# A searched instruction order is replaced by another: engine queues, eviction engines and buffer addresses of a two-branch kernel

## The chip, the cores and the metric

The kernel runs on one core of a Trainium2 chip. The metric is the device time of one execution in microseconds (us), the median of several runs. Inside the core, TensorE (PE) multiplies, VectorE (DVE) and ScalarE (ACT) evict results from the accumulators (PSUM, eight banks) and do elementwise work, GpSimd (POOL) does some elementwise work on the on-chip memory (SBUF), and SyncE (SP) issues nearly all transfers. Each engine works through a queue of its own, strictly in order; semaphores tie the queues together.

## The reference, cut to what matters

Two independent branches over 2048 rows and 576 columns are computed and put side by side.

```python
# branch A: short convolution, product, long convolution over the sequence, gate
k_shift = sum(k_pad[:, t:t+S] * shift_k[:, ks-1-t] for t in range(4))
kv = k_shift * v
y  = irfft(rfft(pad(kv)) * rfft(pad(ssm_k)))[:, :S] + kv * ssm_D
a  = q * y
# branch B: linear attention, 32 heads of 18 columns
qkv = x @ wqkv;  pq, pk = phi(q), phi(k)      # phi(t) = t+1 or exp(t), + 1e-6
o   = (pq @ (pk^T v)) / (pq @ sum(pk) + 1e-6)
b   = o @ wo
out = concat([a, b], axis=-1)
```

## The kernel before, in words

Branch A runs the long convolution as a hand-built Fourier transform in matmuls, in three column pieces (`cc`) of 192, for the filter (`h`) and the data (`u`). Filter columns are transposed on TensorE (`htr`, line 453) and evicted (`hev`); `one1` and `srow` make the four tap rows by matmul (`wjm`, line 314, evicted by `wjev`). VectorE and GpSimd form `kv` (`tap`, `tap+`, `tapv`). `s1` (line 494) is the first transform stage, evicted as 128x768 blocks (`s1ev`, tiles Ch and Cu). Each of the nine 64-column pieces (of the filter and of the data) then has a 32x32-block transpose on VectorE (`tr`, line 533) and two `s2` blocks of eight 32x32-tile matmuls each (line 544): the first block of a piece uses two of the four row groups of the weights, the second the other two. Evictions are 128x1024 (`s2ev`, tiles sph and spu). For each piece a swapped copy X of the filter spectrum is made by two transfers, then come two products of 2048 columns (`p2` on X, `p1` on sph), the inverse stage `i1` (line 590, evicted by `i1ev` into V), a sum and a difference (`vs`, `vd`) and the last stage `i2` (line 633, 24 blocks of four matmuls), whose result is multiplied with q and written out (`yo`); some of these blocks are first copied out of PSUM (`yev`) and then multiplied in SBUF (`yq`), others are multiplied straight out of PSUM (`i2q`).

Branch B projects keys (`k`, line 681, 16 blocks) and queries (`q`, line 703), applies phi in an exponential on ScalarE (`kexp`, `qexp`) and a combination on VectorE (`kphi`, `qphi`), accumulates x^T pk (`G`, line 749; evictions `gcol` and `Gev`), goes through a small chain (`kv`, `z`, `den`, `rden`, a round trip through DRAM `rw`, `rr`) to normalise the queries (`pqn`), folds the output weights into M (line 844), and ends in 16 `out` blocks (line 886; o0 to o7, two of each) that are evicted (`oev`, tile ob) and written out (`oo`). A `fill` (line 921) is two 512-column matmuls on a constant that nobody reads; there are 18.

The order of all this is not written in the Python code. Every operation gets a number as it is declared; the text PLAN lists all 711 numbers, each with the letter of its engine (P, A, D, G for POOL, S for SP), and each engine's queue is the sequence of its words. The text PLACES gives every buffer its SBUF address or PSUM bank in order of declaration. `_issue` reads both:

```python
    for w in PLAN.split():
        o = P.ops[int(w[1:])]
        o.eng = names[w[0]]
        order.append(o)
    ...
    for b, p in zip([b for b in P.bufs if b.space != "dram"], places, strict=True):
        b.pos = p
```

Two rules follow from this. A transfer or a write into an address waits for all earlier users of that address, so PLACES creates waits too. And a two-operand product on GpSimd carries a wait for the last such product that stands before it in VectorE's queue (flag `two`), so that the two engines take turns with products. The three small loads (idw is number 16, Drow 20, srow 23) are declared with ScalarE as their only engine, in the code that both versions share, and they are the first three words of ScalarE's queue in both PLANs (A16, A23, A20).

Numbers that are used below: 360, 357, 355, 352, 350 and so on are `s2` blocks; 693 to 710 fills; 315 the last `out` block and 316 its eviction, 317 its transfer out; 686 and 688 the last `i2` blocks; 489 and 550 the products on X of pieces 2 and 5; 476 and 478 the two `i1` blocks of piece 1; 548 and 549 the two copies X of piece 5; 105 a load of half of q; 480 the sum `vs` of piece 1; 101 a `tapv` of 1536 columns.

Of the kernel before, what the change touches and what calls it, by code (L numbers as in the profile page):

```python
# [946 lines left out]
A16 A23 A20 G692 P697 G10 G5 P708 P706 P695 G7 S318 G218 G0 P702 G24 G8 G71 G1 P321 P25 D26 S324 P701 G3 G12 P319 P29  # L947
P328 G11 P27 P325 S364 S19 D320 A30 A329 A28 P367 P365 P696 D330 D327 A326 G4 D322 S51 P347 D366 P345 D346 A368 P374
A348 A375 P337 A338 G6 G369 P339 G331 S18 D340 P700 G332 G323 P335 P341 D342 A336 P333 P343 A334 P384 P31 D344 D359
D349 G13 P707 A385 P380 S50 P370 G52 A32 P372 A381 S53 P360 A361 G2 D371 S54 P150 P382 A373 G64 S58 S60 A151 G57 S56  # L950
S59 S36 S35 G37 S55 D354 P153 S61 P378 A15 A383 P376 S63 A377 D152 S41 A379 A154 D78 S66 S17 S40 P147 G79 P144 P108
A148 S62 D155 A145 D149 S46 D146 D391 P357 P159 P362 A109 D110 A358 P350 D396 A160 D161 S67 A363 P156 P397 S45 P352
S72 D82 A351 A353 A157 P111 D158 A398 G42 G9 P167 P164 A112 D113 P123 S68 G83 P129 D80 A168 D169 D386 A165 D166 P355
A124 D125 A130 G81 A356 P117 S48 P394 S43 D131 S74 A118 P392 A393 G14 D90 G47 P183 A395 P446 A184 P114 D119 P126 A447
D84 D85 D185 A115 A127 P138 A139 S75 P132 D128 G91 D116 P440 D140 P448 G44 A133 D134 P141 P442 A441 S70 D449 A49 A142
A443 D143 P450 P120 D98 A451 P438 S38 P436 S401 P135 A439 A437 P444 P180 A121 S65 A136 G92 D122 P399 G93 A445 A181
P387 D137 A388 A400 D482 S33 P172 P186 D467 P178 D182 P468 A173 P175 S69 D452 S402 A187 A469 D174 S73 A179 P389 A390
G34 G39 P470 A471 D86 D87 P203 P453 G99 P455 A176 P208 D177 A456 P170 A204 G213 A205 P162 P211 P509 S403 A454 A171
A209 P503 A163 A210 P511 A212 P223 D94 D224 A504 D225 P188 D88 A512 P485 P483 D89 A510 P226 P505 S214 D189 S77 S76
A484 D227 P228 D190 D506 S457 G404 S458 P415 A486 D229 P705 G100 P419 P411 A416 A420 S232 P501 S233 A502 P230 S215  # L960
S473 D412 P497 A498 P499 P507 A508 A500 D95 D96 D97 P191 G101 S472 S487 P413 P417 P409 D231 A192 P206 S488 D528 A414
S239 S241 S243 P405 S22 A410 D207 D459 S237 P558 S246 S245 A418 P407 D474 A408 S217 A559 A406 P193 P560 S234 A561 D489
D475 P568 A194 D460 A195 P566 A567 P198 D242 P531 A569 P529 S216 A199 D421 P196 G244 D543 P562 A532 A530 S235 S252
A197 P422 S250 P424 A200 P201 A425 S248 A423 P570 P564 S254 D490 D563 P544 A202 G238 P220 G240 D426 S548 D513 S256
A571 P546 A565 D222 A545 G219 S533 P572 D221 G236 P429 A547 P709 A430 S580 D573 P266 P516 A267 D431 S534 P262 D517
P476 A263 D604 G249 P698 P260 A477 P434 D435 A261 P264 A265 P258 A259 P427 D574 A428 P493 S519 S518 S247 A494 P461
P463 D462 A464 P268 P478 P432 A269 D589 G251 G253 P575 P279 S549 A479 S107 D433 A576 A280 P491 A492 P285 D536 A286
D257 P592 A593 D255 P514 D535 P270 P300 D551 S106 A515 P605 S610 A271 S579 A301 D465 S287 D520 D521 A606 P607 A608
S594 P273 S595 D480 A274 P282 D481 P590 D495 D550 A283 P577 P294 A591 S302 S609 D596 D611 A578 S281 D496 P524 A525
A295 P297 D582 P522 A298 P537 A538 P288 A523 D597 P539 A540 D612 A289 S21 P276 P552 D526 P554 A277 P306 A553 A555 P613  # L970
P291 A614 S103 A307 S105 S272 P615 S290 A292 D541 S284 S299 S296 D466 P633 D542 A634 D556 P627 P621 P639 P631 P619
S102 S278 A616 D527 D557 A632 P637 A622 D581 P625 S104 A638 G635 A620 P661 D628 P655 P657 S308 D640 P600 D662 D626
A656 P598 S275 A658 P585 S663 A601 D617 P309 S293 P583 D629 D623 S636 A599 S624 D659 S660 D618 D641 A586 S642 D602
P312 S630 D603 P664 A584 P651 D587 D588 P649 A310 S311 D665 D666 P645 P643 A313 A652 A650 A646 S314 A644 P674 S667
# [19 lines left out]
"""  # L994


# [28 lines left out]
```

## Time and profile before

| what | value |
|---|---|
| median of three runs | 153.41 us (152.92 to 153.5) |
| the profiled execution | 153.26 us, of which the span is 151.5 us |
| PE / DVE / ACT / POOL busy | 146.9 / 134.6 / 125.9 / 60.8 us |
| granted TensorE clock | 1.0 |
| transfers | 35.37 MB, mean 234 GB/s |

The span is the time from the first to the last instruction on the trace; about 1.8 us lie outside it. Busy time says how long an engine had an instruction in execution, not whether the engine was the one that others waited for. Matmul records overlap, since matmuls are pipelined; the chain of waits counts each moment once, so its durations of matmul groups are used for what such a group costs. Group lists give the mean duration of one instruction by shape.

### The profile page before, as it was taken

Reading aid. Unit: us, or ns where it says so; the run is one execution under the profiler, and the core shown is the slowest. Engines: PE = TensorE matmul, PEld = TensorE weight load, DVE = VectorE, ACT = ScalarE, POOL = GpSimd, SP = SyncE. Lnnn points to the kernel's source line nnn. Section 1 sums busy time; section 2 is a strip of 40 time slices with the busy share of each in tenths; the row PEclk is TensorE's granted clock in tenths of the full one; section 3 lists DMA queues with packets and bytes.
Section 4 is the critical chain, followed back from the end, with each engine's and each line's share of the span. In section 5 each row is a group of like instructions: output and inputs, shape, how many; then the busy total and the mean of one; then the engine's idle time right before and its main releaser. Section 6 shows DMA issues by size and latency. Waiting matters only on the chain.

```text
span 151.5 us, 4023 instructions
## 1 busy us (share of the span) xinstructions
PE 146.9 (97%) x1627; PEld 110.4 (73%) x1627; DVE 134.6 (89%) x145; ACT 125.9 (83%) x174; POOL 60.8 (40%) x57
## 2 busy tenths in 40 slices
PE   7999999999999999999999999999999999999992
PEld 2568587566768886657867887675777799999970
DVE  0157999999999989999999999999999999999930
ACT  3069888797798788999889879999999999999930
POOL 8107313943911945951063430699940000040200
PEclk9999999999999999999999999999999999999999
DMA  4999999999999791799992776976676796599892
GB/s 132 404 321 254 164 228 286 220 210 176 239 338 296 215 205 34 223 297 196 374 297 57 294 235 162 308 224 253 205 191 262 245 345 169 162 304 244 238 248 89
DMA packets 52629, 35.37 MB, mean 234 GB/s; under 512 B 43328, under 2 KB 48321, under 8 KB 52482
## 3 DMA queue, kind: packets, MB, share of 16 engines
q1 hardware_dynamic: 51918, 33.49, 79.7%
q0 software_dynamic: 544, 1.57, 5.7%
q8 instruction: 13, 0.21, 0.6%
q10 hardware_dynamic: 148, 0.05, 0.2%
q14 instruction: 6, 0.05, 0.1%
HBM read 19.64 MB, written 5.77 MB: 168 GB/s over the span
## 4 chain that ended last, share of the span: by engine, by line
PE 85%; ACT 9%; DVE 2%; issue 2%; POOL 0%; ACTq 0%; POOLq 0%
PE ps_all L681 15%; PE ps_all L703 12%; PE ps_all L886 12%; PE ps_all L749 11%; PE ps_all L494 9%; PE ps_all L921 6%; PE ps_all L590 5%; PE ps_all L633 5%; PE ps_all L544 4%; PE ps_all L453 2%; ACT spu L235 2%; ACT sph L235 2%; PE ps_all L314 2%; ACT Cu L235 1%; ACT M L235 1%
## 5 line engine op out<-in xcount | busy, mean ns | idle before, releaser
L248 POOL TENSOR_TENSOR m<-m 128x3072 bf16<-128x3072 bf16 (+1 forms) x4 | 18.2, 4562 | 14.7 <-DVE m L417 8.6
L681 PE MATMUL ps_all<-wk,xT 128*128 128x324 bf16 x160 | 23.7, 301 | 0.0
L886 PE MATMUL ps_all<-M,pqT 126*128 126x288 bf16 (+1 forms) x160 | 22.1, 287 | 0.1
L681 PEld LDWEIGHTS <-xT 128*128 128x128 bf16 x160 | 17.8, 113 | 4.4 <-issue 0.7
L417 DVE TENSOR_TENSOR m<-kh,Wj 128x6144 bf16<-128x6144 bf16 x6 | 20.1, 3346 | 0.0
L886 PEld LDWEIGHTS <-pqT 126*128 126x128 bf16 (+1 forms) x160 | 17.2, 114 | 2.5 <-issue 1.1
L703 PE MATMUL ps_all<-xT,wq 128*126 128x512 bf16 x80 | 18.7, 382 | 0.0
L494 PEld LDWEIGHTS <-Gsb 128*128 128x128 bf16 x192 | 16.2, 98 | 3.3 <-issue 1.1
L248 POOL TENSOR_TENSOR pqT<-pqT,rb 126x1024 bf16<-126x1024 bf16 (+1 forms) x7 | 14.8, 2133 | 7.7 <-DVE pqT L248 6.5
L235 ACT ACTIVATE spu<-ps_all 128x1024 bf16<-128x1024 f32 x17 | 16.9, 1029 | 0.7 <-PE ps_all L544 0.7
L235 ACT ACTIVATE V<-ps_all 128x1024 bf16<-128x1024 f32 x17 | 17.2, 1116 | 0.0
L235 ACT ACTIVATE Cu<-ps_all 128x768 bf16<-128x768 f32 x20 | 16.3, 858 | 1.1 <-PE ps_all L681 0.6
L749 PE MATMUL ps_all<-pk,x_sb 128*128 128x288 bf16 (+1 forms) x128 | 17.1, 287 | 0.0
L235 ACT ACTIVATE sph<-ps_all 128x1024 bf16<-128x1024 f32 x16 | 15.9, 1023 | 1.1 <-PE ps_all L544 0.8
L235 ACT ACTIVATE Ch<-ps_all 128x768 bf16<-128x768 f32 x18 | 14.3, 852 | 1.9 <-PE ps_all L494 1.8
L703 PEld LDWEIGHTS <-wq 128*126 128x126 bf16 x80 | 10.4, 136 | 6.4 <-issue 1.1
L749 PEld LDWEIGHTS <-x_sb 128*128 128x128 bf16 x128 | 12.1, 98 | 3.8 <-issue 0.9
L686 ACT ACTIVATE ek<-ps_all,neg 128x648 bf16<-128x648 f32 x16 | 12.4, 806 | 2.8 <-PE ps_all L681 2.7
L248 POOL TENSOR_TENSOR q<-yb,q 128x768 bf16<-128x768 bf16 (+1 forms) x2 | 2.6, 1280 | 29.4 <-DVE yb L237 22.2
L689 DVE SCALAR_TENSOR_TENSOR pk<-ek,ps_all 128x648 bf16<-128x648 bf16 x16 | 12.7, 823 | 0.8 <-ACT ek L686 0.8
L921 PE MATMUL ps_all<-cft 128*128 128x512 bf16 x36 | 11.4, 449 | 1.0 <-POOL cft L915 1.0
L235 ACT ACTIVATE ob<-ps_all 128x576 bf16<-128x576 f32 x16 | 10.4, 724 | 1.9 <-PE ps_all L886 1.7
(95 smaller groups left out, 299.5 us busy)
## 6 DMA issues: line engine op xcount, KB each, us to landing
X<-sph SPq DMA_DIRECT2D x18, 256.0 KB
kh<-in_A_k_dram SPq DMA_DIRECT2D x6, 384.0 KB
v<-in_A_v_dram SPq DMA_DIRECT2D x6, 384.0 KB
x_sb<-in_B_x_dram SPq DMA_DIRECT2D x4, 576.0 KB
q<-in_A_q_dram SPq DMA_DIRECT2D x6, 384.0 KB
out_dram<-ob SPq DMA_DIRECT2D x16, 144.0 KB
out_dram<-q SPq DMA_DIRECT2D x11, 192.0 KB
rb<-r_scr SPq DMA_DIRECT2D x8, 252.0 KB
```

The costliest lines, as they stand in the source:

```text
L235: nc.scalar.activation(out=o, in_=i, func=ACTF.Copy)
L248: return (nc.vector if e == "DVE" else nc.gpsimd).tensor_tensor(out=o, in0=a, in1=b, op=op)
L417: return nc.vector.tensor_tensor(out=m.t[:], in0=i0, in1=i1, op=ALU.mult)
L494: nc.tensor.matmul(ps.t[:, bank, lo - 384 * bank:hi - 384 * bank], lhsT=Gsb.t[:, b, ri, :], rhs=src[:, lo - CC * j:hi - CC * j], start=Tru ...
L590: nc.tensor.matmul(view(ps.t[:], 128 * c + 16 * wi, [[32, 4], [1, 16]]), lhsT=src.t[:, 4 * h0 + c, :], rhs=Ei.t[:, 0, 64 * wi:64 * wi + 64 ...
L681: nc.tensor.matmul(ps.t[:, hh, 0:KH], lhsT=cols(xT.t[0:KT[t], t, :], r), rhs=wk.t[0:KT[t], t, KH * hh:KH * hh + KH], start=(t == 0), stop= ...
L686: P.op("A", lambda e: nc.scalar.activation(out=eb.t[:], in_=ps.t[:, :, 0:KH], func=ACTF.Exp, bias=neg1.t[:]), rd=[ps, neg1], wr=[eb], name ...
L689: P.op("D", lambda e: nc.vector.scalar_tensor_tensor(out=pk[r // 4].t[:, r % 4, 0:2 * KH].rearrange("p (h c) -> p h c", h=2), in0=eb.t[:], ...
L703: nc.tensor.matmul(ps.t[0:hn, c - c0, :], lhsT=wq.t[0:KT[t], t, HCH[c][0]:HCH[c][0] + hn], rhs=xT.t[0:KT[t], t, :], start=(t == 0), stop=( ...
L749: nc.tensor.matmul(ps.t[0:m, 0, 0:n], lhsT=x4[r // 4].t[:, r % 4, :] if t == 4 else x_sb[r // 4].t[:, r % 4, 128 * t:128 * t + 128], rhs=p ...
L886: nc.tensor.matmul(ps.t[:, hh - h, 0:HALF], lhsT=cols(pqT[r // 8].t[0:hn, c, 512 * (r // 4 % 2):512 * (r // 4 % 2) + 512], r), rhs=M.t[0:h ...
L921: nc.tensor.matmul(fps.t[:, 0, :], lhsT=cft.t[:], rhs=view(cft.t[:], 0, [[0, 4], [1, 128]]), start=True, stop=True)
```

## The change

Both texts are replaced; no other line changes. The same 711 operations are issued, on the same data and with the same shapes. What differs is the order inside each engine's queue, the engine of 40 operations, and the buffer addresses. The lines that matter most, cut:

```diff
 PLAN = """
-A16 A23 A20 G692 P697 G10 G5 P708 P706 P695 G7 S318 G218 G0 P702 G24 G8 G71 G1 P321 P25 D26 S324 P701 G3 G12 P319 P29
-P328 G11 P27 P325 S364 S19 D320 A30 A329 A28 P367 P365 P696 D330 D327 A326 G4 D322 S51 P347 D366 P345 D346 A368 P374
...
-P476 A263 D604 G249 P698 P260 A477 P434 D435 A261 P264 A265 P258 A259 P427 D574 A428 P493 S519 S518 S247 A494 P461
...
-S594 P273 S595 D480 A274 P282 D481 P590 D495 D550 A283 P577 P294 A591 S302 S609 D596 D611 A578 S281 D496 P524 A525
...
-D653 D647 P680 D681 P682 P676 P670 S654 P688 P686 D675 A683 S648 A677 A689 P303 P668 P315 P694 G684 A671 S685 D678
-P703 D690 D672 D687 A304 S679 S691 P693 S305 D669 S673 P704 A316 S317 P710 P699
+G692 P700 G10 P701 P702 P696 D24 S318 G3 G71 P707 A16 G6 A23 S324 S19 P321 G12 P29 S364 D322 S51 D30 P319 P697 P328
+P31 A20 G57 D329 P325 D330 D326 A320 G323 S18 G331 G1 S50 D327 G64 A32 P706 P339 A340 S53 P337 S54 S58 P345 P367 A346
...
+P476 P434 D435 P478 P709 P266 A477 A479 P427 S252 S105 S549 S247 A267 P546 A428 A547 S548 D589 P461 D462 P268 A269
...
...
+D628 D629 A671 P682 P676 S305 S314 D669 P674 D672 D681 P688 A683 A677 D684 A665 P686 A689 S630 S673 S685 P315 D675
+D678 D687 D690 D666 S679 S691 S667 D316 P693 P699 P703 P698 P710 P694 P704 S317
```

The operations that change engine:

| from, to | operations |
|---|---|
| ACT to DVE | `hev` 3, `wjev` 2, `oev` 2 (277 and 316), `Gev` 2, `yev` 2, `gcol`, `s2ev` of u (545), `s1ev` of h 2 |
| DVE to ACT | `s1ev` of h 5, `s1ev` of u 2 (449 and 563), `yev` 3, `Gev` 2, `hev` |
| DVE to POOL | `p2` (489), `vs` (480), `pqn` 2, `yq` |
| POOL to DVE | `tapv` (101), `one1` (24), `pqn` 2, `yq` 2 (635, 684) |
| ACT to POOL | `x4c` (a small copy) |

The `s2` blocks stand in TensorE's queue, from first to last, in these groups without other work between:

```
before: 360 | 357 | 362 350 | 397 352 | 355 | 394 392 | 399 387 | 468 | 389 470 | 453 455 | 485 483 | 531 529
        | 422 424 | 544 | 546 | 429 | 516 | 434 | 427 | 432 575 | 592 514 | 605 607 | 590 577
after:  360 357 | 362 350 | 397 352 | 394 392 | 355 | 399 387 | 470 468 | 389 453 | 483 455 | 485 | 531 424 529
        | 544 422 | 429 | 516 | 434 | 427 546 | 432 | 607 514 | 592 590 | 605 | 577 575
```

Of the fills, twelve stand ahead of the last `out` block before and eleven after; five open TensorE's queue in both.

More of the change, by code (lines that the diff above doesn't have):

```diff
@@ L952 @@
[L952 to L961, printed above, removed]
@@ new lines @@
+A398 G83 A157 P352 P167 D158 S63 A353 A168 P129 P123 A130 D80 D169 P164 S48 D386 A124 P111 G5 G81 D131 D125 A165 P446
+G14 D166 P117 P394 A112 A447 D113 P392 A393 S45 A395 P183 P438 A118 D90 P114 S75 D119 D84 S74 A439 D85 A184 P355 G47
+D185 P126 A356 G91 A115 G49 D116 A127 D128 P132 S43 A133 S401 P138 A139 P448 A449 S73 D134 P141 D140 G13 A142 P440
+A441 D143 P444 P120 P450 P442 A445 D98 A451 P135 A443 S70 P436 G92 A15 G93 G9 A121 A136 A437 P180 P399 A181 D122 P387
+A388 D137 D467 P172 P705 D452 A400 S33 S38 S72 A173 P470 D182 D482 S69 D174 D86 P468 A471 S402 P175 P389 A469 P453
@@ new lines @@
+P592 D574 S533 A283 P590 A289 P276 A593 P605 A591 D277 G480 P306 P577 A606 A307 S107 P575 S519 A576 S594 P554 P270
+P291 A555 A271 P552 S102 D535 P294 D596 D536 A578 D520 A292 D481 D495 D521 A553 A295 S579 D556 S609 P537 A538 P539
+A540 S21 P309 P522 S284 D597 A310 S610 A523 P524 A525 D581 D582 P463 S103 D557 S281 A464 P297 S290 S278 D526 S106 P300
+S104 D496 D465 P600 A298 P585 D466 A301 P285 A586 P583 S311 P631 A601 D611 A584 S296 P633 S293 P273 A632 A634 A286
+S299 S302 S272 D541 S287 D527 D542 D612 P639 D587 P661 P637 P621 A640 A274 D635 A638 P598 D622 S275 P655 P657 P649
```

29 lines of the change are left out of this document (15 added, 14 removed), and 30 rows, old and new, of the table PLACES.

## The prediction, on record before the result

> **What bounds the kernel now.** I read the page first (busy shares), then busy time in stretches, then the chain of waits, then the groups by shape.
>
> ```profile
> span 151.5 us, 4023 instructions
> ...
> PE 146.9 (97%) x1627; PEld 110.4 (73%) x1627; DVE 134.6 (89%) x145; ACT 125.9 (83%) x174; POOL 60.8 (40%) x57
> ```
>
> ```profile
> 16.00:76.00 60.00, 59.97 (x524) 42.69 (x523) 59.01 (x49) 51.96 (x68) 28.75 (x18) 1.00 1.01 231
> 76.00:100.00 24.00, 23.56 (x292) 18.11 (x291) 23.83 (x25) 21.04 (x31) 10.60 (x5) 1.00 0.73 230
> 100.00:144.00 44.00, 43.69 (x679) 37.42 (x678) 43.72 (x62) 43.30 (x64) 14.01 (x9) 1.00 0.76 235
> ```
>
> The columns of the stretches are length, then busy time (and instructions) of PE, PEld, DVE, ACT and POOL, the clock, the share of the transfer engines and GB/s. From 16 to 144 us VectorE works 126.6 of 128 us: it has no slack. ScalarE has 8.0 us of slack up to 76, 3.0 in the next 24 and only 0.7 in the last 44. TensorE is busy throughout too, but a busy PE may be one whose next matmul is held back, so I take its share from the chain of waits (start, duration, what):
>
> ```profile
> 1.01 4.45 PE ps_all L921 x10
> ...
> 26.48 0.34 PE ps_all L544 x8
> ...
> 29.12 0.36 PE ps_all L544 x16
> ...
> 65.65 0.55 PE ps_all L544 x16
> ...
> 144.49 0.33 PE ps_all L633 x4
> 144.82 1.24 PE ps_all L886 x10
> 146.06 2.59 PE ps_all L921 x12
> ```
>
> The real work of TensorE begins behind the first fills, at 5.46, and ends at 146.06; the last 2.59 us of fills delay nobody. So three engines are nearly full at once, and no single one can be relieved to great effect. A new order can win only what lies in waits, in fills ahead of 146.06, and in the way blocks follow each other.
>
> **The change part by part.** The work is the same, so I count what the order does to each queue. All sums are against the profiled execution (153.26 us: the span of 151.5 and 1.76 around it); it lies 0.15 below the median of 153.41, so 0.15 is added at the end.
>
> *TensorE, the s2 blocks.* A block of eight alone takes 0.34 us. Two neighbours that use different row groups take 0.36 together (29.12); two that use the same row groups take 0.55 (65.65: blocks 389 and 470, both second halves). In the old order ten blocks stand alone, eleven pairs mix halves and two pairs (389 470, 432 575) do not: 10 x 0.34 + 11 x 0.36 + 2 x 0.55 = 8.46 us. In the new one seven stand alone, twelve pairs mix, one pair (544 422) does not, and three stand in a row (531 424 529: 0.55 + 0.03, since the third mixes with the second): 7 x 0.34 + 12 x 0.36 + 0.55 + 0.58 = 7.83. That removes **0.63 us** where TensorE sets the pace, nothing where it waits anyway; I take it whole, as it is spread over the run.
>
> *TensorE, the fills.* A fill is 2.59 / 6 = 0.43 us. Eleven stand ahead of the last out block, one fewer: **-0.43 us**, if the fill filled no wait; if it did, 0. The seven at the end take 3.0 us behind block 315 and end before the last transfer lands, so they cost nothing.
>
> *VectorE.* The prices are the mean ns in these groups:
>
> ```profile
> L248 DVE TENSOR_TENSOR X<-spu,X 128x2048 bf16<-128x2048 bf16 x9 | 11.1, 1263 | 0.0
> ...
> L237 DVE CAST Ch<-ps_all 128x768 bf16<-128x768 f32 x6 | 5.6, 940 | 0.8 <-PE ps_all L494 0.7
> L248 DVE TENSOR_TENSOR VS<-V 128x896 bf16<-128x896 bf16 x9 | 5.5, 616 | 0.0
> ...
> L248 DVE TENSOR_TENSOR v<-m,v 128x1536 bf16<-128x1536 bf16 x3 | 2.9, 959 | 0.1
> L248 DVE TENSOR_TENSOR q<-ps_all,q 128x384 bf16<-128x384 f32 x5 | 2.7, 552 | 0.2
> L237 DVE CAST sph<-ps_all 128x1024 bf16<-128x1024 f32 x2 | 2.4, 1178 | 0.0
> ...
> L248 DVE TENSOR_TENSOR q<-yb,q 128x384 bf16<-128x384 bf16 x4 | 1.3, 367 | 0.0
> ...
> L237 DVE CAST Wj<-ps_all 128x576 bf16<-128x576 f32 x1 | 0.8, 758 | 6.8 <-PE ps_all L314 6.8
> ```
>
> Behind the first block transposes, where VectorE is full, it loses two Ch evictions (371, 412; 2 x 0.94), two of Cu (449, 563; the same shape as Ch), p2 489 (1.26), vs 480 (0.62) and one yev net (128x384 from PSUM, 0.55 as the q row), 6.2 us. It gains one spu eviction (545, priced as the sph row, 1.18), two of ob (277, 316; 128x576 from PSUM as Wj, 2 x 0.76), tapv 101 (0.96) and 0.37 us of yq, 4.0 us. Small ones (gcol, Gev, pqn) cancel within 0.2. Net **about -2 us of VectorE work**. The additions ahead of the transposes (one1, two wjev, two hev net, against two s1ev) lie ahead of 16 us, where at most 134.6 - 126.6 = 8 us of VectorE's work stands; I take 0 for them, with 0 to +0.4 as bounds, since the transposes there wait for the last eviction of s1 and one more wjm block (0.6) now stands before that, and one htr block is taken later.
>
> *ScalarE.* An ob eviction is this row:
>
> ```profile
> L235 ACT ACTIVATE ob<-ps_all 128x576 bf16<-128x576 f32 x16 | 10.4, 724 | 1.9 <-PE ps_all L886 1.7
> ```
>
> In the full last 44 us ScalarE gives away two of these (1.4) and one 128x1024 eviction (at most the 1.18 of the row above), and takes one 128x768 (at most 0.94) and one 128x384 (at most 0.55): about 1 us less, bounds 0.5 to 1.5. The rest of its changes lie earlier, in its slack.
>
> So where waits are made, both evicting engines have 1 to 2 us less to do. What TensorE stood waiting for them shows in the stretch 76 to 100, where 0.44 us is idle, and in 100 to 144, 0.31 us; a block held back counts as busy, so the true loss may be larger, and I bound the gain between 0 and 1.4 (the lesser of ScalarE's and VectorE's relief at its upper end). I take **-0.4**, near the rows' low end.
>
> *GpSimd.* It takes p2 489 and vs 480 and gives tapv 101 away. By this row p2 (2048 columns) is 4.27 us and vs (896) 1.87:
>
> ```profile
> L248 POOL TENSOR_TENSOR pqT<-pqT,rb 126x1024 bf16<-126x1024 bf16 x6 | 12.6, 2134 | 1.2 <-DVE sph L248 1.2
> ```
>
> Product 489 must wait for VectorE's product 460, and six pqn (12.8 us, with a memset) stand behind it. For such places I sum the durations ahead of an operation in the new queue and look where the old one had done as much; for 460 that is within the first of these rows, at about 89 us:
>
> ```profile
> 87.93 3.93 DVE L248 TENSOR_TENSOR X<-spu,X 128x2048 bf16<-128x2048 bf16 x3
> ...
> 109.59 1.22 DVE L533 STREAM_TRANSPOSE ct<-Cu 128x1024 f32<-128x1024 f32 x1
> ...
> 120.97 3.49 DVE L248 TENSOR_TENSOR X<-spu,X 128x2048 bf16<-128x2048 bf16 x3
> ```
>
> So 489 ends at some 94.5, the pqn of the first half at 106, the rest at 110. The out blocks that need them are reached at about 109 and 115: covered by 3 to 5 us, cost 0; a slip of 460 by more than 3 us would come through one for one. The POOL row has six products of one length beside whatever VectorE did. A rule of the Trainium skill speaks against the move all the same, GPSIMD Engine Reference, section 1 (Specifications): the SBUF interfaces are shared, and VectorE instructions with two SBUF inputs contend with GpSimd. By that rule the move of p2 could cost up to the time it had on VectorE, an estimate of +1.3 us; no row here shows products of both engines side by side for long, and the sum goes without it.
>
> *SyncE.* Several loads change places: v1, kh1 and kh2 pieces come earlier, x2 transposes and x_sb later. The transfer engines are full up to 76 us (1.01), and by the shapes of three loads (126, 384 and 576 KB) about 1.1 MB more stands ahead of the last x transposes, 4.8 us at 231 GB/s; their first reader, a k block, has over 40 us of PE work ahead of it. Cost 0, bounds 0 to 1. A second shift is the q load 105 (below).
>
> *The end.* The old end:
>
> ```profile
> 146.15 0.65 ACT L235 ACTIVATE ob<-ps_all 128x576 bf16<-128x576 f32 x1 [0.97 <-PE ps_all L886]
> 147.12 0.46 SPq L228 DMA_DIRECT2D out_dram<-ob  x1
> ```
>
> Now VectorE does this last eviction behind its last products. From the start of the last eight i2 blocks, TensorE needs 8 x 0.33 + 1.24 = 3.88 us. VectorE, starting when two of the blocks are done (0.7), needs 4 x 0.55 + 5 x 0.37 = 4.05, so 316 starts at 4.8 and ends at 5.5, 1.6 us behind TensorE; before it was 146.80 - 146.06 = 0.7, and the transfer waited 0.3 more on SP. That is 0 to +0.7; I take **+0.3**.
>
> Sum: -0.63 - 0.43 - 0.4 + 0.3 = **-1.16 us**, 152.1 against 153.26; against the median 152.25, say **152.2**.
>
> **The rivals.**
>
> *VectorE alone sets the pace.* For it: 126.6 of 128 us. Against: TensorE's blocks in the chain rows follow each other without a gap there (144.49, 144.82, 146.06). Then the -2 us of its work come through whole, with the end's +0.3: 153.41 - 1.7 = **151.7 us**. The Trainium skill, Perfetto Trace Analysis, section Identifying the Most-Contended Engine, points this way: it judges PE by its weight loads (73% here), not by matmul time, and the others by occupancy, where VectorE leads with 89%. The trace agrees with it on VectorE, but TensorE's gapless end does not look like an engine with a quarter of its time free. Chance 0.12.
>
> *ScalarE sets the pace from 100 us on, or the order is as good as the old one.* For it: 43.3 of 44 us, and PE's blocks there alternate over few PSUM banks, so that each waits for the eviction two before. VectorE then runs ahead and waits for ScalarE's evictions. The savings on PE are then waits under another name: within -0.5 and +0.6 of the old time, **153.4 us**. Chance 0.28.
>
> *Slower: the copies of piece 5 come late.* In the old order the second of them was issued at 107.22 and used at 120.97, by product 550, the first of the three in the row above. The second row here is 476, an i1 block:
>
> ```profile
> 107.22 0.47 SPq L228 DMA_DIRECT2D X<-sph  x1
> ```
>
> ```profile
> 103.47 0.20 PE L590 MATMUL ps_all<-Ei,sph 128*128 128x64 bf16 x1
> ```
>
> Now both copies (549, 548) stand on SP behind q load 105, whose address is free only once i1 block 478 is done, and product 550 stands 10 us earlier in VectorE's queue, with all later products behind it. 478 now has as much PE work ahead of it as 476 had, which started at 103.47; four issues of some 0.5 us and 0.5 MB at 235 GB/s (2.2) later it is 108. 550's place was reached at 110, in the transpose of 109.59. That is 2 us spare, less what VectorE is ahead. If 478 comes at 106 or later (it waits for evictions of ScalarE's), VectorE stands; 3 us of standing against the 2 saved, with the end's +0.3, gives 153.41 + 1.3 = **154.7 us**. Chance 0.2.
>
> **How the numbers follow.** My forecast has 0.4. About 0.5% (0.77 us) is what a measurement of this kernel can tell from no change: faster is below 152.64, slower above 154.18. Faster: nearly all of the forecast (0.36) and of the first rival (0.12) give 0.48. Slower: 0.2 from the third rival and 0.02 from the second. The rest, 0.3, is the same. The range reaches from 151.4 (first rival with its bounds) to 154.6, which leaves out most of the far end of the slow case; the forecast's own is 151.6 to 152.9.
>
> **What would show it.** Right: real PE work ends near 145 instead of 146.06; s2 groups of 16 at 0.36 rise from eleven to twelve or more; VectorE's busy time in 16 to 144 keeps its share but its queue ends at the last eviction, about 1.6 us behind PE's last out block; 489 ends before 96. Wrong: VectorE idle on a transfer into X near 110; idle on ScalarE near 120 to 130; PE waits over 1 us anywhere between 16 and 140.

## The result, and the profile after

The changed kernel takes **167.36 us** (median of four executions, 165.61 to 171.59) against 153.45 us (152.92 to 153.59) of the kernel before on the same chip. The ratio is 1.0818, with a 95% interval of 1.0763 to 1.0873; this and all ratios below leave disturbed executions out, the medians don't. The prediction was 152.2 us with a range to 154.6: wrong in sign and by 15 us.

The page of the profiled execution (171.59 us, span 169.8) has the same 1627 matmuls in it. TensorE, VectorE and ScalarE are busy within 2.4 us of before, GpSimd 10.5 us longer (71.3 against 60.8), and the span is 18.3 us longer. In the rows of 40 slices (4.2 us each here) TensorE falls to 0 in the thirteenth and fourteenth, and the bytes that move fall well before that, from the tenth on:

```profile
span 169.8 us, 4019 instructions
...
PE 149.3 (88%) x1627; PEld 110.9 (65%) x1627; DVE 135.1 (80%) x148; ACT 125.1 (74%) x171; POOL 71.3 (42%) x57
...
PE   7999999999920079999469999999999999999994
...
GB/s 172 392 255 278 165 236 227 257 241 85 66 92 48 49 319 171 191 330 163 101 281 116 260 202 172 250 76 168 244 269 343 317 304 351 275 93 177 290 198 109
```

The stretches (columns as in the prediction) put the loss ahead of 100 us. From 16 to 76 TensorE, VectorE and ScalarE each have 12 to 15 us less work behind them than before, from 76 to 100 another 3 to 5 us less; TensorE's granted clock falls to 0.91 as it stands. Up to 76 us the transfer engines are nevertheless reported as full (1.11), at 178 GB/s where 231 were moved before. From 100 to 144 us TensorE and VectorE are as busy as before:

```profile
16.00:76.00 60.00, 47.16 (x378) 32.89 (x375) 44.26 (x39) 39.52 (x49) 27.88 (x17) 0.91 1.11 178
76.00:100.00 24.00, 20.40 (x222) 14.35 (x221) 18.47 (x16) 17.14 (x26) 15.00 (x10) 0.93 0.73 190
100.00:144.00 44.00, 43.70 (x631) 34.34 (x629) 43.72 (x46) 42.12 (x59) 21.19 (x10) 1.00 0.77 246
```

The waits between 36 and 64 us (engine and line, what it waited for, us, times, longest) name two transfers. TensorE stands for the transposed x, `xT`, and VectorE for the adding transfer, `m<-m`; ScalarE waits for TensorE and GpSimd for VectorE in turn:

```profile
POOL m L248 <- DVE v L248: 21.5, 1, 21.5
ACT ek L686 <- PE ps_all L681: 16.0, 3, 15.4
DVE m L248 <- DMA m<-m: 14.6, 1, 14.6
...
PE ps_all L681 <- DMA xT<-in_B_x_dram: 12.7, 1, 12.7
```

The chain of waits goes through SyncE's queue into one transfer of 25.87 us. It is load 45 (line 365), which brings 512 rows of x transposed into the third `xT`:

```profile
33.16 0.58 SPq L228
...
33.79 0.71 SPq L228
...
34.54 25.87 DMA xT<-in_B_x_dram
...
60.45 4.42 PE ps_all L681 x20
```

The other transfer is operation 83 (line 423), issued by GpSimd 0.2 us earlier: within SBUF, it adds two of the four taps of one convolution piece to the other two (768 KB). The list of issues (the last number is us from issue to landing) has it at 25.9 us, where the kernel before has 8.4, one line each, of the kernel after and then of before:

```profile
m<-m POOLq DMA_DIRECT2D x1, 768.0 KB, 25.9
```

```profile
m<-m POOLq DMA_DIRECT2D x1, 768.0 KB, 8.4
```

So two transfers that need about 2.5 and 4.4 us of packets in the old kernel share 22 us in the new one (called the jam below). What moved between 40 and 50 us, after and then before, shows that it is no lack of demand: the transfer engines are reported as busy throughout and move less than a quarter of the bytes.

```profile
DMA packets 828, 0.67 MB, mean 67 GB/s; under 512 B 665, under 2 KB 665, under 8 KB 828
...
q1 hardware_dynamic: 659, 0.17, 65.6%
q0 software_dynamic: 169, 0.50, 53.2%
```

```profile
DMA packets 3501, 2.90 MB, mean 290 GB/s; under 512 B 3061, under 2 KB 3061, under 8 KB 3499
```

By the trace's packet records, a 256-byte packet of load 45 took 0.107 us in the mean (0.022 before), a 3072-byte packet of 83 took 0.498 (0.253 before). VectorE stood from 45.6 and TensorE from 47.7 us; both transfers crawled on to 60 beside idle engines.

A second, smaller wait follows in this execution. From 82 to 87 us TensorE stands 3.6 us for GpSimd's copies into `x` (128x256, line 239). The second and third of these copies take 5.33 us together, where the kernel before has 0.74. The lines are of the kernel after (its waits, then two rows of its timeline) and then of before:

```profile
PE ps_all L749 <- POOL x L239: 3.6, 3, 1.5
```

```profile
79.27 3.36 DVE L417 TENSOR_TENSOR m<-kh,Wj 128x6144 bf16<-128x6144 bf16 x1 [0.47 <-POOL v L248]
```

```profile
79.42 5.33 POOL L239 COPY x<-x_sb 128x256 bf16<-128x256 bf16 x2
```

```profile
64.65 0.74 POOL L239 COPY x<-x_sb 128x256 bf16<-128x256 bf16 x2
```

The jam has put these copies behind the start of VectorE's products with two inputs in SBUF. A copy that begins with no such product running takes 0.39 to 0.41 us in every kernel here; each of the four of this execution began beside one, took 1.44 to 3.60 us, and ended 0.24 to 0.26 us behind the end of a VectorE product. The two waits of 12.7 and 3.6 us make up 16.3 of the 18.3 us. The profiled execution is the longest of the four; whether the other three have the second wait isn't known.

### The profile page after: what moved, and what is told of

It reads as the page before. It is cut to its first block, busy times and chain, and to the rows that moved or that the text cites. A ratio compares the mean times of both kernels' runs of the same rounds, so it can differ in the third digit from the quotient of the medians.

```text
span 169.8 us, 4019 instructions
## 1 busy us (share of the span) xinstructions
PE 149.3 (88%) x1627; PEld 110.9 (65%) x1627; DVE 135.1 (80%) x148; ACT 125.1 (74%) x171; POOL 71.3 (42%) x57
## 4 chain that ended last, share of the span: by engine, by line
PE 53%; DMA 23%; SPq 9%; ACT 5%; POOL 5%; DVE 2%; issue 1%; ACTq 0%
DMA xT<-in_B_x_dram 15%; PE ps_all L886 10%; PE ps_all L749 9%; PE ps_all L681 8%; PE ps_all L494 6%; PE ps_all L590 4%; DMA h_scr<-hr 4%; SPq L228 4%; DMA kh<-in_A_k_dram 4%; PE ps_all L633 4%; POOL x L239 4%; SPq L365 3%; PE ps_all L703 3%; PE ps_all L544 3%; SPq L367 2%; PE ps_all L921 2%
## 5 line engine op out<-in xcount | busy, mean ns | idle before, releaser
L681 PE MATMUL ps_all<-wk,xT 128*128 128x324 bf16 x160 | 25.5, 311 | 12.8 <-DMA xT<-in_B_x_dram 12.7
L248 POOL TENSOR_TENSOR m<-m 128x3072 bf16<-128x3072 bf16 (+1 forms) x4 | 18.3, 4566 | 32.5 <-DVE v L248 21.5
L686 ACT ACTIVATE ek<-ps_all,neg 128x648 bf16<-128x648 f32 x16 | 12.4, 801 | 16.7 <-PE ps_all L681 16.6
L235 ACT ACTIVATE Cu<-ps_all 128x768 bf16<-128x768 f32 x22 | 18.2, 851 | 5.5 <-PE ps_all L494 5.4
L248 DVE TENSOR_TENSOR m<-m 128x1536 bf16<-128x1536 bf16 (+1 forms) x6 | 7.4, 1237 | 14.7 <-DMA m<-m 14.6
L235 ACT ACTIVATE Ch<-ps_all 128x768 bf16<-128x768 f32 x21 | 16.7, 851 | 2.4 <-PE ps_all L494 2.3
L749 PE MATMUL ps_all<-pk,x_sb 128*128 128x288 bf16 (+1 forms) x128 | 17.1, 287 | 0.0
L235 ACT ACTIVATE spu<-ps_all 128x1024 bf16<-128x1024 f32 x16 | 15.8, 1031 | 0.4 <-PE ps_all L544 0.4
L689 DVE SCALAR_TENSOR_TENSOR pk<-ek,ps_all 128x648 bf16<-128x648 bf16 x16 | 12.7, 822 | 1.1 <-ACT ek L686 1.1
L494 PE MATMUL ps_all<-v,Gsb 128*128 128x192 bf16 x96 | 11.4, 251 | 0.0
```

The lines of the kernel that those rows point to most:

```text
L235: nc.scalar.activation(out=o, in_=i, func=ACTF.Copy)
L248: return (nc.vector if e == "DVE" else nc.gpsimd).tensor_tensor(out=o, in0=a, in1=b, op=op)
L494: nc.tensor.matmul(ps.t[:, bank, lo - 384 * bank:hi - 384 * bank], lhsT=Gsb.t[:, b, ri, :], rhs=src[:, lo - CC * j:hi - CC * j], start=Tru ...
L681: nc.tensor.matmul(ps.t[:, hh, 0:KH], lhsT=cols(xT.t[0:KT[t], t, :], r), rhs=wk.t[0:KT[t], t, KH * hh:KH * hh + KH], start=(t == 0), stop= ...
L686: P.op("A", lambda e: nc.scalar.activation(out=eb.t[:], in_=ps.t[:, :, 0:KH], func=ACTF.Exp, bias=neg1.t[:]), rd=[ps, neg1], wr=[eb], name ...
L689: P.op("D", lambda e: nc.vector.scalar_tensor_tensor(out=pk[r // 4].t[:, r % 4, 0:2 * KH].rearrange("p (h c) -> p h c", h=2), in0=eb.t[:], ...
```

## The experiments

Load 45's and transfer 83's packets, first to last, in us of the profiled execution of each kernel; how many of load 45's 2048 packets were still to begin when the first of 83 began; and the median time:

| kernel | load 45 | transfer 83 | still to begin | us (executions) |
|---|---|---|---|---|
| before | 33.85 to 36.35 | 38.59 to 43.02 | 0 | 153.45 (4) |
| after | 37.71 to 59.75 | 38.94 to 59.47 | 1631 | 167.36 (4) |
| e1, 45 earliest | to 33.39 | 37.43 to 41.72 | 0 | 153.71 (13) |
| e2, 83 held back | 37.24 to 39.44 | 39.16 to 43.36 | 46 | 153.52 (8) |
| e3, 83 an addition on GpSimd | 37.07 to 39.21 | none | | 156.81 (2) |
| e4, before with 45 behind 75 | 38.68 to 44.07 | 37.98 to 42.21 | 2048 | 153.85 (2) |
| f1, 45 two places earlier | to 36.27 | 37.06 to 41.70 | 0 | 152.22 (12) |
| f2, before with 45 behind 74 | 36.65 to 38.61 | 38.54 to 42.14 | 25 | 153.15 (10) |
| f3, 45 one place later | 39.18 to 59.83 | 39.52 to 58.86 | 1990 | 161.45 (4) |
| g2, 83 a plain copy | 37.97 to 51.81 | 38.57 to 51.23 | 1930 | 159.31 (4) |
| g3, 45 not transposing | 37.71 to 45.16 | 38.43 to 44.21 | 1610 | 152.37 (10) |
| g1, f1 and one store on ScalarE | to 36.66 | 36.51 to 40.95 | 37 | 151.89 (6) |

Where the row says "to", the packets of load 46, which are alike, run straight into those of 45. The diffs below give SyncE's words of PLAN alone where only its order changes.

**e1: load 45 earliest.** T1 was that the transposing load and the adding transfer hold each other up, T2 that only the bytes ahead of load 45 make it late, T3 that the new addresses do.

```diff
-S40 S68 S67 S62 S46 S63 S48 S45 S75 S74
+S40 S46 S45 S68 S67 S62 S63 S48 S75 S74
```

> The new order with one step moved on SyncE: the two transposing loads of x2 (46 and 45) stand right behind load 40, ahead of six ordinary loads, as they did in the old order; all else is the new order. T1 (the transposing load and the adding transfer 83 hold each other up when they run at the same time): load 45 lands at or before about 38 us instead of 60, transfer 83 lands within 9 us of its issue instead of 26, the long waits at 56 to 64 and 82 to 87 us are gone, and the time is 151.5 to 154; where it comes out in there is what the rest of the change is worth, which the prediction put at 152.2. T2 (only the bytes that stand ahead of load 45 make it late): the same for load 45, but six loads of some 1.5 MB land up to 5 us later than now, so the time is 153 to 156, and transfer 83 still takes over 15 us, since the queues are as full as before. T3 (the new places in memory make the transposing load slow wherever it stands): load 45 still takes over 20 us from issue to landing, and the time stays above 160.

Measured: 153.71 us, ratio to before 1.001 (0.9989 to 1.0032); transfer 83 took 8.5 us. The 14 us are gone, so T3 is out; 83 ran undisturbed in a queue as full as before, against T2. The rest of the change looked worth nothing here, but load 62 had come behind: in the profiled execution (155.75 us, a long one) GpSimd's product stood 3.0 us for it, TensorE 2.3 for that product; whether the shorter executions have that wait isn't shown. One execution of the thirteen took 161.34 us, and there is no profile of it.

**e2: transfer 83 held back.** SyncE's order stays.

```diff
-A398 G83 A157 P352 P167 D158 S63 A353 ... S48 ... S45 ... P355 G47
+A398 S63 S48 S45 G47 G83 A157 P352 P167 D158 A353 ... P355
```

> The new order on SyncE unchanged, so that the same loads stand ahead of the transposing load 45; only the adding transfer 83 on GpSimd is placed behind a memset that has to wait for the landing of load 45, so the two cannot overlap. T1: load 45 lands within 9 us of its issue (at about 42 to 45 us instead of 60), transfer 83 begins there and lands by about 53, ahead of the 60 of now; the time is 152 to 157. T2: load 45 still lands near 60, transfer 83 only at about 68, and the time is 166 to 174.

Measured: 153.52 us, ratio 1.0004 (0.9971 to 1.0036), so T2 falls: the same loads ahead, and load 45 lands in time. But the expectation misdescribed the edit. The memset waits for load 46, not 45, so 83 was issued only 1.5 us later (35.81), and its packets met the last 46 of load 45's. That was enough. One wait of TensorE remained, as GpSimd's product started late:

```profile
40.60 0.49 PE L494 MATMUL ps_all<-v,Gsb 128*128 128x192 bf16 x4 [0.94 <-POOL v L248]
```

**e3: the addition on GpSimd.**

```diff
-ACC = [(0, 1), (2, 1)]
+ACC = [(2, 1)]
```

> The new order with the first adding transfer (83) made an addition on GpSimd (about 6 us of that engine for 128x3072 elements); the second stays a transfer. SyncE's order is unchanged. T1: load 45 lands within 9 us of its issue instead of 26, PE's wait for it is under 2 us instead of 12.7, and the time is 152 to 157 (GpSimd's 6 us may be felt). T2: load 45 still takes 20 us or more, since the same bytes stand ahead of it, and the time stays at 163 or more.

Measured: 156.81 us, ratio 1.0223 (1.0179 to 1.0267), load 45 undisturbed, as T1 has it. What the edit loses against the kernel before comes through VectorE: its sum of 128x1536 of another piece began at 34.51, while GpSimd's addition ran (33.54 to 39.54), and took 5.84 us where the other sums of that shape take 0.95. The phi behind it came late, and TensorE stood 3.6 us for it.

**e4: the old kernel with load 45 later.**

```diff
-S46 S67 S45 S72 S68 S48 S43 S74 S75 S70
+S46 S67 S72 S68 S74 S75 S45 S48 S43 S70
```

> The kernel before with one step moved on SyncE: the transposing load 45 stands behind loads 72, 68, 74 and 75, so that it is issued after the adding transfer 83 has begun. Nothing else of the change is in it. T1: load 45 takes 15 to 26 us from issue to landing instead of 5, transfer 83 15 to 25 instead of 8, and the time is 158 to 168. T2: load 45 lands 4 to 6 us later than now, transfer 83 is as before, and the time is 153 to 154.5, since the first k block that reads it has PE work ahead of it.

Measured: 152.39 and 155.32 us, transfer 83 8.8 us. T1's number missed. The table says why the run doesn't contradict it: 83's packets came 0.7 us ahead of load 45's, and some 1900 of those 2048 began only behind 42 us, as 83 ran out. Overlap alone isn't what hurts; T1 was narrowed to T1b, that 83 has to come into the middle of a running stream of transposing packets.

**e5: the transfers alone.**

```diff
+PHASES = ["T", "A", "TA", "C", "TC", "AL", "TL"]
```

> The transfers by themselves, with no other work: nothing of the computation is done, and only a few elements of the output are written. Seven phases, each begun when the one ahead has landed: T, the transposing loads of 512 rows of x; A, the adding transfer of 768 KB within SBUF on GpSimd's queue; TA, both at once; C, the same transfer without the addition; TC, transposes with it; AL, the adding transfer with an ordinary load of 384-byte rows; TL, transposes with that load. T1 in its narrow form (transposing and adding collide): T takes 4 to 8 us, A 6 to 9, TA 18 to 26, all others no more than the sum of their two parts. T1 in a wide form (any transfer on GpSimd's queue collides with transposes): TC takes 18 to 26 as well. T1 in the widest form (a transposing load is slow beside any transfer): TL too takes more than the sum. T2: TA, TC, AL and TL each take at most the sum of their two parts, 10 to 16 us.

Measured, from the first issue to the last landing: T 5.9, A 6.5, TA 9.6, C 3.8, TC 6.6, AL 7.1, TL 7.3 us. Every form of T1 that was written down falls as stated: side by side, issued together, the pair takes less than its sum. In TA the adding packets came between the packets of the two transposing loads, not into one of them.

**f1: load 45 two places earlier.**

```diff
-S40 S68 S67 S62 S46 S63 S48 S45 S75 S74
+S40 S68 S67 S62 S46 S45 S63 S48 S75 S74
```

> The new order with one step moved on SyncE: the transposing load 45 stands in front of loads 63 (v) and 48 (x), two places earlier, and everything else as changed. Theory T1b (what the first runs leave of T1: the transfers jam only when the adding transfer 83 comes into the middle of the stream of transposing packets, not when one follows the other): the stream of load 45 runs from about 34.5 to 37.5 us, 83 begins near 39, so there is no jam; and load 62, which GpSimd's product on v needs, is no later than in the changed kernel, so the 0.9 us for which PE waited on that product in the run with transfer 83 held back, and the 2.3 in the run with load 45 earliest of all, are gone. If the terms of the prediction other than SyncE's were right, the time is 152.0 to 152.8; if the new order is worth nothing without the jam, 153.2 to 153.8.

Measured: **152.22 us**, ratio 0.9926 (0.9895 to 0.9957): faster than before. This kernel is the change without the collision, and it is used below to check the other steps of the prediction.

**f2: the collision in the old kernel.**

```diff
-S46 S67 S45 S72 S68 S48 S43 S74 S75 S70
+S46 S67 S72 S68 S74 S45 S48 S43 S75 S70
```

> The kernel before with the transposing load 45 moved behind loads 72, 68 and 74, one load less far than in the run where it stood behind 75 as well. There its packets began 0.7 us after those of the adding transfer 83, and followed them. Here they should begin near 36.7 us and 83 near 38, in their middle. T1b: jam in the old kernel too: load 45's packets last over 8 us instead of 2.5 and 83's over 8 instead of 4.4, time 156 to 168, or, where the two miss each other in a run, 153. T2 (backlog) and T3 (the new places in memory): no jam, 152.5 to 154.

Measured: nine executions at 152.16 to 155.89, one at 167.99 us. In the profiled one the adding packets came with 25 of load 45's left, so the aim was missed. One long execution in ten is what T1b allows for a near miss, but it has no profile.

**f3: load 45 one place later.**

```diff
-S40 S68 S67 S62 S46 S63 S48 S45 S75 S74
+S40 S68 S67 S62 S46 S63 S48 S75 S45 S74
```

> The new order with the transposing load 45 still later, behind load 75. T1b: its packets begin after those of transfer 83 and follow them (as in the old kernel with load 45 behind 75), load 45 lands at 43 to 46, its first reader on PE stands at about 47.5, so there is no wait and the time is 152.5 to 154.5: later is 12 us faster. T2: load 45 lands later than now, time 166 to 170. T3 (places in memory): still over 160.

Measured: 154.9, 156.8, 166.11 and 166.8 us. The expectation of no wait was missed. The edit doesn't fix the order of the two: in the profiled execution (166.11) load 45's packets came 0.34 us ahead of 83's, not behind them, and the two jammed, with 25.2 us for 83. One place in the queue moves the start of load 45's packets by 1.5 us (39.18 against 37.71). Two of the four times lie near 155 us and two near 166, so the same kernel seems to fall on either side from one execution to the next; only the one has a profile.

**e6: mixed at other moments.** The transposing loads are two of 512x512; the columns of a memset on GpSimd set the delay.

```diff
+PHASES = [("T", 0), ("A", 0), ("TA", 512), ("TA", 1024), ("TA", 1536), ("TC", 1024), ("LA", 1024), ("TAw", 1024)]
```

> Transfers by themselves again (nothing of the computation is done, and only a few elements of the output are written), now with the adding transfer of 768 KB begun about 0.5, 1 and 1.5 us later than two transposing loads of 512x512 each, so that it comes into the middle of their packets; then a plain copy in its place, ordinary loads in the transposes' place, and the middle case with VectorE and GpSimd multiplying beside it. T1b with the pair alone as the cause: the three mixed phases take 15 to 25 us against about 6 for the transposes and 7 for the addition alone; the plain copy or the ordinary loads in one of the two places stay at 8 to 12. If engines at work are needed as well: only the last phase takes over 15. If something else of the kernel is needed (other loads in the queue behind): none does, and all stay at 9 to 13.

Measured: T 6.7, A 6.6, the mixed three 11.5, 10.6 and 10.8, TC 8.2, LA 8.8, with engines at work 11.1 us. No jam. In all of them the adding packets began as the first transposing load's ran out, and ahead of the second's (for one, they began at 67.97 us, the first load's packets ended at 68.22, and the second's began at 69.81), so again none came into the middle of one load: 17 to 171 of the first load's 2048 packets were still to begin.

**g2 and g3: which of the two has to be what it is.** Here the changed kernel keeps its order, and one of the two transfers becomes another kind. Both diffs are shortened.

```diff
-                out=..., in_=..., accum_op=ALU.add, max_dma_last_dim=3072),
+                out=..., in_=..., max_dma_last_dim=1536, **(dict(accum_op=ALU.add) if cc else {})),
```

> The changed kernel with transfer 83 a plain copy of the same bytes within SBUF instead of an adding one: the addition of two of the four taps of one piece is left out of the computation. All places and orders are those of the changed kernel. If the jam needs the addition: load 45 lands within 9 us of its issue and the time is 151.5 to 155. If any transfer of GpSimd's queue within SBUF jams with the transposing packets: load 45 still takes over 15 us, time 160 to 172.

Measured: 159.31 us (158.01 to 159.7), ratio 1.0331 (1.0265 to 1.0397), and the copy took 17.1 us:

```profile
m<-m POOLq DMA_DIRECT2D x1, 768.0 KB, 17.1
```

The addition isn't needed. The jam lasts 22 us with it and 13.8 without, but the copy also went in 176 packets of 4608 or 3072 bytes instead of 256 of 3072, so the addition alone need not make the difference. (The edit halves the packets of the second adding transfer too, which runs later.)

```diff
-            load("xT", b, lambda e: nc.sync.dma_start_transpose(out=b.t[:, 0:4, :], in_=x[...]), ...)
+            load("xT", b, rows if g == 2 else lambda e: nc.sync.dma_start_transpose(...), ...)
+            # rows: for c in 0..3 an ordinary load of 512 pieces of 256 bytes into b.t[:, c, :]
```

> The changed kernel with load 45 made four ordinary loads of the same bytes in the same 256-byte pieces to the same place, so that the rows of x that it brings are not transposed (the third quarter of x is left in the wrong order, and what is computed from it is not the reference's). If the jam needs the transposing load: no jam, the bytes land within 9 us and the time is 151.5 to 155. If any 256-byte packets jam with the adding transfer, the time is 160 to 172.

Measured: 152.37 us, ratio 0.9915 (0.9882 to 0.9948). The 2048 pieces of 256 bytes started at 37.71 us, where load 45's had, 83 came into their middle at 38.43, and both were through by 45.16: 7.5 us, near the 2.5 and 4.4 of the two alone. The transposing load is needed.

**e7: the queue around the two, alone.** The number is the columns of GpSimd's memset ahead of the adding transfer, "b" the loads behind.

```diff
+PHASES = [("Ab", 900), ("Ab", 1800), ("Ab", 2500), ("Ab", 3200), ("Ab", 3900), ("Ab", 4600), ("Ab", 5300),
+          ("A", 1800), ("A", 2500), ("A", 3200), ("A", 3900), ("A", 4600)]
```

> Transfers by themselves once more (nothing of the computation is done, and only a few elements of the output are written), now with what stands around load 45 in the changed kernel: a load of v, a load of x, the transposing load of 512x512, then in seven phases two loads of kh behind it, in five more none; GpSimd begins the adding transfer 0.8 to 4.7 us after them, in steps of 0.6. If the queue around the two is the missing part, one or more of the phases whose adding transfer comes into the middle of the transposing packets take over 18 us, among those with loads behind or among all; the others take 9 to 14. If something else of the kernel is needed, all take 9 to 14.

Measured: the jam, with no other engine at work. Each pair of rows is the issue of the adding transfer and VectorE's copy that waits for its landing; the pairs are the second and fourth phase (loads behind) and the eighth and ninth (none):

```profile
35.77 1.21 POOL L59 DMA_DIRECT2D m<-m  x1
54.91 0.16 DVE L48 COPY scr<-m 128x1 bf16<-128x1 bf16 x1 [20.76 <-DMA m<-m]
...
82.08 1.21 POOL L59 DMA_DIRECT2D m<-m  x1
90.59 0.16 DVE L48 COPY scr<-m 128x1 bf16<-128x1 bf16 x1 [11.29 <-DMA m<-m]
...
137.57 1.21 POOL L59 DMA_DIRECT2D m<-m  x1
156.95 0.16 DVE L48 COPY scr<-m 128x1 bf16<-128x1 bf16 x1 [21.00 <-DMA m<-m]
...
159.75 1.21 POOL L59 DMA_DIRECT2D m<-m  x1
168.66 0.16 DVE L48 COPY scr<-m 128x1 bf16<-128x1 bf16 x1 [11.11 <-DMA m<-m]
```

It takes 19.1 and 19.4 us where the two jam, 8.5 and 8.9 where they don't. The three earliest delays of seven jam, and the earliest of five without loads behind. In those four phases 961 to 1923 of the 2048 transposing packets were still to begin when the adding ones came; in the eight others 32 to 93. So what the pair needs is the moment, and neither the loads behind nor engines at work. The table above has the same divide: a jam with 1631 to 1990 packets still to begin, none with 46 or fewer, and none in e4, where load 45 hadn't begun at all.

**g1: the last store on ScalarE's queue.** f1 with one letter changed.

```diff
-D316 P693 P699 P703 P698 P710 P694 P704 S317
+D316 P693 P699 P703 P698 P710 P694 P704 A317
```

> The run with load 45 in front of 63 and 48, and one step more: the last output transfer (317) is issued by ScalarE instead of SyncE. This tests the term of the prediction for the end, +0.3 us, which was put down to VectorE's late last eviction (316). In the run with load 45 in front, 316 ended at 145.40 and the transfer was issued only at 146.69, since SyncE was still issuing six others. If SyncE's queue is what the end waits for, the transfer is issued near 145.5 and the time falls by 0.6 to 1.2 us, to 151.0 to 151.7. If the end hangs on the six other transfers or on VectorE, the time stays at 152.0 to 152.5.

Measured: 151.89 us (151.62 to 152.69), ratio 0.9872 (0.983 to 0.9913). That is the lowest median of all, between the two expectations, and its interval overlaps that of f1. The store was issued at once, but the span fell by only 0.4 us, to 149.9: the stores of `q` end no earlier, and their last packets are then what the end waits for.

```profile
145.50 0.37 ACTq L228 DMA_DIRECT2D out_dram<-ob  x1
```

## Why the prediction was wrong, by its own steps

**SyncE: the step that failed.** It read "Cost 0, bounds 0 to 1" for the later x transposes. The measured cost is that of f1 against the changed kernel, 167.36 - 152.22 = 15.1 us. The shift itself was well sized: 4.8 us was the estimate, and load 45's packets began 3.9 us later (37.71 against 33.85). What the step left out is what else runs at the new moment. It counted bytes and looked for the reader, and it did not look at GpSimd's queue, past which the load was moved: transfer 83 had its packets at 38.59 in the old trace, and 33.85 + 4.8 is 38.65. Both numbers were there to be put side by side. What such a meeting costs was not there: the old trace has no instance.

The cover was misread as well. "Over 40 us of PE work ahead" was counted from the kernel's start; the reader stands at 47.7 us, 13 us after the load's issue. That was enough for a load of 5 us, and for one of 25.87 it left 12.7 of waiting.

Two rules of the Trainium skill would have seemed to support the failed step. DMA: Bandwidth & Descriptors, section Rules for kernel authors, says that a transposing transfer next to ordinary ones needs nothing. The row is about wrong data and says nothing of time; for time, this load needed to be kept apart from a transfer within SBUF (167.36 us against 152.22), and the measurement decides. The same page, section Queues, rings and completion order, has each transfer engine take turns between its queues packet by packet. By that the two would be through in about the sum of their packets' times alone, 2.5 + 4.4 = 6.9 us, an estimate from this case's records. g3 agrees, with 7.5; the changed kernel, with 22, does not.

**The other steps, on f1.** Without the collision the forecast of 152.2 meets 152.22 us. The parts are less exact than the sum, so that the two agree this closely is in part luck. The stretches of f1, with 0 to 16 first, and the end of its chain:

```profile
0.00:16.00 16.00, 14.99 (x117) 9.29 (x118) 7.83 (x14) 8.22 (x10) 5.69 (x21) 1.00 0.93 278
16.00:76.00 60.00, 59.88 (x539) 43.22 (x537) 58.51 (x49) 52.84 (x70) 32.24 (x24) 1.00 1.03 230
76.00:100.00 24.00, 23.71 (x299) 18.66 (x299) 23.39 (x25) 21.63 (x31) 14.13 (x7) 1.00 0.64 198
100.00:144.00 44.00, 43.36 (x661) 37.21 (x661) 43.69 (x59) 42.25 (x63) 12.71 (x8) 1.00 0.85 262
```

```profile
104.20 0.66 PE ps_all L544 x16
...
143.25 1.23 PE ps_all L886 x10
144.48 3.02 PE ps_all L921 x14
```

TensorE's real work ends at 144.48 instead of 146.06: -1.58, where -0.63 - 0.43 - 0.4 = -1.46 was forecast.

- The fills: 22 of the 36 matmuls stand ahead of the last out block, 24 before. One fill fewer, as forecast. The 0.43 us are taken from a fill's length; the run doesn't show them apart.
- The s2 blocks: 21 groups as forecast, but from a group's start to the next other work they take 9.00 us in all against 9.19 before, waits behind them included, so -0.19 instead of -0.63. Prices of 0.34 to 0.55 don't hold for all groups: the pair 427 546 takes 0.66 (the first row of the chain above), 544 422 takes 0.80. A mis-sized term.
- The relief of VectorE and ScalarE: what is left of -1.58 is -0.96, where -0.4 was taken and -1.4 was the bound. In the last 44 us ScalarE has 42.25 us of work instead of 43.30, -1.05 as forecast. VectorE has 125.59 us in 16 to 144 instead of 126.56, -1.0 and not -2. A fixed stretch says little of an engine that is full in both kernels, but durations agree: from the first block transpose on (16.7 us in both) VectorE's instructions add up to 135.4 us against 136.6, -1.2. The work ahead of it grew by 1.5 us, for which the forecast took 0; it had counted two `s1ev` evictions as gone there, and one is. Which single wait gave the 0.96 wasn't tried.
- The end: from TensorE's last out block to the end of the span 150.3 - 144.48 = 5.82 us, against 151.5 - 146.06 = 5.44: +0.38, forecast +0.3. The reason given was half right. VectorE ends the last eviction 0.9 us behind TensorE (forecast 1.6), and the store then stands 1.3 us in SyncE's queue behind stores of `q`:

```profile
144.49 2.11 SPq L228 DMA_DIRECT2D out_dram<-q  x2
144.65 0.75 DVE L237 CAST ob<-ps_all 128x576 bf16<-128x576 f32 x1
...
146.69 0.44 SPq L228 DMA_DIRECT2D out_dram<-ob  x1
```

- GpSimd: product 489 ends at 93.97 (forecast 94.5), the normalised queries at 102.3 and 109.3 (106 and 110; seven products, where the forecast counted six). Cost 0 for these, right. While 489 runs, VectorE has a reciprocal, a copy and transposes and no product out of SBUF, so its move says nothing on the price of two engines on SBUF, for which the prediction had an estimate of +1.3:

```profile
89.89 4.08 POOL L248 TENSOR_TENSOR X<-spu,X 128x2048 bf16<-128x2048 bf16 x1 [9.87 <-DVE sph L248]
93.92 8.39 POOL L248 TENSOR_TENSOR pqT<-pqT,rb 72x1024 bf16<-72x1024 bf16 x4
```

  Where products of both engines meet, the price shows. VectorE's products of 128x2048 on X take 1.21 to 1.23 us, and 1.42 in f1 for the one that ran into the moved `vs` 480 (1.66 before for one that ran into a `tapv`). A product of 128x768 took 0.88 us in f1, where the other five take 0.55; GpSimd's product ran from 134.00 to 135.65, and f1's chain of waits goes through this row:

```profile
135.18 0.88 DVE L248 TENSOR_TENSOR q<-yb,q 128x768 bf16<-128x768 bf16 x1
```

  The copies of the changed kernel and VectorE's sum in e3 (above) are larger cases of the same.

**The rivals.** None of the three gives f1's time, though its chain runs through VectorE's queue from 134.01 to 140.45 us, as the first had it for the whole kernel. The slower one, VectorE standing for the copies of piece 5 near 110 us, didn't: it works 43.69 of 44 us there in f1. VectorE alone as the pace would have been 151.7, and ScalarE from 100 us on 153.4; f1's 152.22 lies between, and its interval (0.9895 to 0.9957, 151.9 to 152.8 us) leaves both out, the first only just. The signs that were named beforehand did show the failure, though not the place: a wait of TensorE over 1 us between 16 and 140.

**What stays open.** That a transposing load whose packets are running when this transfer within SBUF begins makes both slow is shown in the changed kernel's order and alone; that it needs no addition and no engine at work is shown as well. In the old kernel's order it isn't: f2 missed the moment, and its one long execution has no profile. In every run the transfer within SBUF was issued by GpSimd, so which of the two matters, the place or the queue, wasn't tried. How the transfer engines come to the jam isn't known, nor how many packets must be left: 171 did no harm (in e6), 961 did (in e7), and no run fell between. The long execution of e1 is open too, since in its profiled one 4 us lie between the two transfers.

## What to carry to other kernels

When a transfer is moved, put its new moment beside every other transfer that runs then, on all queues, GpSimd's too; a sum of bytes and a far reader don't cover a meeting of two kinds. Keep transposing loads clear of transfers that GpSimd issues within SBUF, best with the transposing load through first: f1, with 0.8 us between the two in its profile, stayed below 152.8 us in all twelve executions, and f3, which aimed the load behind the transfer by its place in the queue alone, did not hold that order. A product on GpSimd is not free for VectorE either: ask which VectorE products it will stand beside. And when a large edit loses, undo its pieces one at a time: here one word of 711 held 15 us, and the rest was a gain.

## What the runs showed of the hardware that was not expected

- A transposing load of 512x512 (2.2 to 2.5 us of packets) and a transfer of 768 KB within SBUF (4.4 us) took 22 us when the second came into the first, 13.8 us when the second only copied (in other packets), and 7.5 us when the first did not transpose. The transfer engines were reported as busy all the while, at 67 GB/s.
- The jam needs no engine: it held for 12 us beside an idle TensorE, and came in the run of transfers alone (19.1 and 19.4 us).
- TensorE's granted clock fell to 0.91 and 0.93 in the two stretches in which it stood, and was 1.00 after.
- GpSimd's instructions and VectorE's products with two inputs in SBUF held each other up for whole instructions: a copy of 0.40 us took up to 3.60 and ended 0.26 us behind VectorE's product, and a VectorE sum of 0.95 us took 5.84 beside GpSimd's addition (e3).
